# Batch 0's second half of the queries: loaded behind the keys, mixed around the first scores

## The chip, the cores and the metric

The kernel runs on one core of one Trainium2 chip. The metric is the device time in microseconds (us) of one execution; three executions of the kernel before are known, and one more was taken with the hardware profiler. The core has five engines that run side by side and wait for each other by semaphores: TensorE (PE; its weight loads are listed apart as PEld), VectorE (DVE), ScalarE (ACT), GpSimd (POOL) and SyncE (SP). DMA transfers are issued by POOL, by SP and, once, by ACT.

## The reference

Attention within blocks, with keys and values whose blocks were first mixed by a matrix that is normalized by rows and columns five times, and behind it a gated feed-forward network without an expert choice:

```python
P = sort_net                                   # 4 x 8 heads x 8 x 8 blocks
for _ in range(5):
    P = P - max(P, -1); P = exp(P)
    P = P / (sum(P, -1) + 1e-09)
    P = P / (sum(P, -2) + 1e-09)
k_sorted = einsum('bhij,bhjcd->bhicd', P, k_b)  # v_sorted likewise; blocks of 96 rows
scores = q_b @ k_sorted_b.T / sqrt(64)
attn = softmax(scores)
x = (attn @ v_sorted_b), heads side by side     # 3072 x 512
out = (silu(x @ w_gate) * (x @ w_val)) @ w_out  # d_ff 1536
```

q, k and v are 4 x 8 x 768 x 64 in float32; the kernel computes in bfloat16 and accumulates in float32.

## The kernel before

**Stages.** The 3072 output rows are worked in eight pieces `n` of 384 rows (two for each batch). For each piece there are 12 pairs of `gate` and `value` (four matmuls each over 384 columns) and the output matmuls `outp` of the piece before. Between these, PE's order has the attention work of coming pieces: the mixing of keys and queries into their transposed form (`kq_chunk`, for batch 0 `k0_chunk` and `q0_chunk`), the mixing of values (`v_chunk`), the scores (`scores`, 16 small matmuls, followed by exponentials on ACT in `exps`), the product with the values (`av`, whose result is divided on DVE: `r_sb` and `st`) and a transposition (`x_to`).

**Order.** Up to the first two gate and value pairs everything runs in an order written out by hand on PE, POOL, DVE and ACT (first `manual_schedule`): what stands earlier in the program is executed earlier on its engine. After that PE, POOL, ACT and SP keep the written order, which `merge` makes from a list of costs and due times, and DVE is ordered by the framework.

**The start.** POOL issues the loads of batch 0: the values in two halves (`load_v(0, ...)`), the first half of the queries (`load_q0(0)`; a half `t` is four of the eight blocks, in a layout of 128 partitions by 24 rows), and the keys in two halves (`k0`). Then it makes its share of the value copies (`copy_v`), which put the values in an order by head dimension into `vch`. ACT makes the rest of these copies between its exponentials of the five normalizing rounds. POOL then issues the gate and value weights in four column ranges (`load_gv`), with the second half of the queries, `load_q0(1)`, behind the first range, and both halves of batch 1's values; later come three mixing products on POOL (`mix_rows`), four tiny memsets to `pad`, batch 1's keys and queries in halves and the output weights.

**PE's order of the start.** 105 tiny matmuls and some `fill`s (matmuls of zeros with 512 columns), the transposition of the mixing matrix (`w_ps`), `q0_chunk(0, ...)` and `v_chunk(0, ...)` in turns, `k0_chunk`, then the first four scores and value products with single fills between them, the first two gate and value pairs in pieces (`early`), and `q0_chunk(1, ...)`, which mixes the second half of the queries in chunks of 16 and 8. These queries are first read by the fifth score unit, `qk(0, 4)`, which stands behind three more gate and value steps.

**Banks and drains.** A chunk's result stands in a PSUM tile. Tag `gen` has three single banks that are given out in turn, `x` one bank, `a` and `b` two banks each. A chunk ends with a `drain`, a cast to bfloat16 by ACT (`"s"`) or DVE (`"v"`), as the call says:

```python
def q0_chunk(t, at, n, eng, tag):
    ...
    for lc in range(n):
        for two in range(2):
            nc.tensor.matmul(tp[two * D:(two + 1) * D, lc], lhsT=q0[t][:, at + lc, :],
                             rhs=sel[:, two], start=True, stop=True)
    drain(eng, dst[:, :, :, at:at + n], tp.rearrange("p l g r -> p g r l"))
```

A chunk of 8 is 16 matmuls and a drain of 512 columns, a chunk of 16 is 32 matmuls and a drain of 1024 columns.

## Time and profile before

| | |
|---|---|
| three executions | 247.69, 244.64 and 244.58 us, median 244.64 |
| the profiled execution | 244.79 us, of which 243.0 us are the span from its first to its last instruction |
| PE busy | 233.1 us (96% of the span) |
| DVE, ACT, POOL busy | 154.9, 112.5, 54.0 us |
| PE busy from 0 to 12 us | 8.51 us |
| PE busy from 12 to 18 us, and from 18 to 24 us | 5.71 and 5.37 us |
| PE busy from 30 to 60 us | 29.79 us |
| granted TensorE clock | 1.00 |

A time in the profile counts from the first instruction. The views used below are the 40 slices (busy tenths of every engine), the chain of work that ended last in order of time, the timeline (each line: start, duration, engine, line, operation, tiles, count; in brackets the idle time before it and what ended it), and tables by stretches of time (busy time of each engine, granted clock, share of the 16 DMA engines that is busy, and GB/s). Durations of PE are modelled ends, so that neighbouring matmuls overlap in the list.

### The profile page before, as it was taken

How to read it: one execution, taken by the hardware profiler on the slowest of the kernel's cores; microseconds unless marked ns; L12 is line 12 of the kernel's file. 1: busy time of each engine (PE TensorE's matmuls, PEld its weight loads, DVE VectorE, ACT ScalarE, POOL GpSimd, SP SyncE). 2: the span in 40 equal slices, each digit the busy share in tenths (PEclk: the TensorE clock that was granted, in tenths of full speed). 3: DMA queues.
4: the chain of work that ended last, by engine and by line, in shares of the span. 5: the costliest groups of instructions: out<-in, count | busy, mean ns of one | idle time of the engine just before them, and what ended most of it. 6: DMA issues, size and time to landing. Idle time of an engine off the chain costs nothing.

```text
span 243.0 us, 6137 instructions
## 1 busy us (share of the span) xinstructions
PE 233.1 (96%) x2587; PEld 138.8 (57%) x2611; DVE 154.9 (64%) x325; ACT 112.5 (46%) x191; POOL 54.0 (22%) x54
## 2 busy tenths in 40 slices
PE   7799999999999999999999999999999999999993
PEld 5376665676556556555565565565556555555543
DVE  6696889775666585776855765484566477444700
ACT  3987662576525444455454253345226433333221
POOL 5996328970006098000000000000000000000000
PEclk9999999999999999999999999999999999999999
DMA  5999999999926997462122112012102211110122
GB/s 95 211 123 184 207 212 211 206 210 200 182 79 126 203 182 116 95 134 61 42 71 65 35 43 80 0 59 63 44 31 61 60 36 43 43 43 3 43 86 86
DMA packets 40698, 24.77 MB, mean 102 GB/s; under 512 B 29408, under 2 KB 35424, under 8 KB 40672
## 3 DMA queue, kind: packets, MB, share of 16 engines
q0 software_dynamic: 20688, 14.16, 39.8%
q1 hardware_dynamic: 19840, 10.17, 15.9%
q8 instruction: 20, 0.33, 0.6%
q10 hardware_dynamic: 144, 0.07, 0.1%
q14 instruction: 6, 0.05, 0.1%
HBM read 28.32 MB, written 7.86 MB: 149 GB/s over the span
## 4 chain that ended last, share of the span: by engine, by line
PE 90%; DVE 4%; DMA 2%; issue 1%; ACT 1%; DVEq 0%; POOLq 0%
PE v_ps L428 25%; PE g_ps L410 25%; PE o_ps L445 24%; PE av_ps L359 3%; PE tkq L264 3%; PE qk L332 3%; DMA v<-in_v_dram 2%; PE tv L310 1%; PE o_ps L461 1%; PE tv L300 1%; DVE vt L242 1%; PE tk L284 1%; DVE h L433 1%; PE g_ps L561 1%; PE idle_ps L477 1%
## 5 line engine op out<-in xcount | busy, mean ns | idle before, releaser
L420 DVE SCALAR_TENSOR_TENSOR gs_sb<-th_sb,g_ps 128x384 bf16<-128x384 bf16 x96 | 52.9, 552 | 50.3 <-ACT th_sb L418 47.3
L410 PE MATMUL g_ps<-xt,wg_sb 128*128 128x384 bf16 x376 | 76.6, 325 | 0.1
L428 PE MATMUL v_ps<-xt,wv_sb 128*128 128x384 bf16 x376 | 76.5, 326 | 0.0
L418 ACT ACTIVATE th_sb<-g_ps 128x384 bf16<-128x384 f32 x96 | 47.1, 491 | 56.9 <-PE g_ps L410 54.2
L445 PE MATMUL o_ps<-wo,h 128*128 128x512 bf16 x254 | 61.4, 379 | 1.5 <-issue 0.5
L433 DVE SCALAR_TENSOR_TENSOR h<-v_ps,gs_sb 128x384 bf16<-128x384 f32 x96 | 53.4, 556 | 7.8 <-PE tq L274 0.5
L428 PEld LDWEIGHTS <-wv_sb 128*128 128x128 bf16 x376 | 35.0, 97 | 23.1 <-issue 0.2
L410 PEld LDWEIGHTS <-wg_sb 128*128 128x128 bf16 x376 | 34.9, 97 | 23.4
L445 PEld LDWEIGHTS <-h 128*128 128x128 bf16 x276 | 26.1, 98 | 28.5
L450 ACT COPY o_sb<-o_ps 128x512 f32<-128x512 f32 x23 | 13.5, 586 | 49.3 <-PE o_ps L445 49.3
L148 POOL COPY vch<-v 64x1536 bf16<-64x1536 bf16 (+2 forms) x11 | 28.8, 2662 | 9.5 <-PE g_ps L410 7.5
L345 ACT ACTIVATE e_all<-qk 96x768 bf16<-96x768 f32 x30 | 23.2, 801 | 4.3 <-PE qk L332 4.3
L365 DVE TENSOR_TENSOR st<-av_ps,r_sb 96x512 bf16<-96x512 f32 x32 | 21.8, 680 | 0.3
L359 PEld LDWEIGHTS <-e_all 96*128 96x128 bf16 x256 | 12.0, 98 | 4.9 <-ACT e_all L345 0.7
L359 PE MATMUL av_ps<-vt,e_all 96*128 96x65 bf16 x256 | 13.0, 193 | 0.4 <-ACT e_all L345 0.4
L244 ACT CAST vt<-tv 96x1024 bf16<-96x1024 f32 (+1 forms) x11 | 10.1, 931 | 4.4 <-PE tv L310 3.5
L363 DVE RECIPROCAL r_sb<-av_ps 96x8 f32<-96x8 f32 x32 | 6.4, 199 | 7.9 <-PE av_ps L359 7.9
L242 DVE CAST vt<-tv 96x1024 bf16<-96x1024 f32 (+1 forms) x7 | 7.5, 1065 | 1.9 <-PE tv L310 1.8
L242 DVE COPY oq_v<-o_ps 128x128 f32<-128x128 f32 x1 | 0.3, 292 | 9.3 <-PE o_ps L461 9.3
L477 PE MATMUL idle_ps<-warm_sb 128*128 128x512 bf16 x20 | 5.7, 384 | 0.5 <-issue 0.5
L395 POOL DMA_DIRECT2D q_scr<-in_q_dram x2 | 5.6, 2813 | 0.3 <-issue 0.3
L146 ACT COPY vch<-v 64x768 bf16<-64x768 bf16 (+1 forms) x4 | 5.4, 1374 | 0.3 <-DMA v<-in_v_dram 0.3
(89 smaller groups left out, 133.0 us busy)
## 6 DMA issues: line engine op xcount, KB each, us to landing
out_dram<-o_sb SPq DMA_DIRECT2D x23, 256.0 KB, 2.0
v<-in_v_dram POOLq DMA_DIRECT2D x4, 384.0 KB, 12.3
wo<-in_moe_w_out_dram POOLq DMA_DIRECT2D x3, 512.0 KB, 16.2
kqp<-in_k_dram POOLq DMA_DIRECT2D x2, 768.0 KB, 9.8
q_scr<-in_q_dram POOLq DMA_DIRECT2D x2, 768.0 KB, 17.2
v<-in_v_dram POOLq DMA_DIRECT2D x2, 768.0 KB, 9.3
wg_sb<-in_moe_w_gate_dram POOLq DMA_DIRECT2D x2, 512.0 KB, 12.3
wv_sb<-in_moe_w_val_dram POOLq DMA_DIRECT2D x2, 512.0 KB, 14.5
```

Source lines behind the costliest of these rows:

```text
L148: eng.tensor_copy(dst, src.transpose([0, 2, 1]))
L242: nc.vector.tensor_copy(dst, src)
L345: nc.scalar.activation(e_all[:, n:n + 2, 0:4 * C], wide[0:C, :, 0:4 * C], AF.Exp, scale=scale)
L359: nc.tensor.matmul(o[:, two, i4, 0:D + 1], lhsT=e[:, i4 * C:i4 * C + 128], rhs=vt[:, 2 * g + two, half * 4 + i4, 0:D + 1], start=True, sto ...
L365: nc.vector.tensor_tensor(st.rearrange("p i two d -> p two i d"), o[0:C, :, :, 0:D], r_sb.to_broadcast([C, 2, 4, D]), op=ALU.mult)
L410: nc.tensor.matmul(g_ps, lhsT=wg_sb[:, kc, ts(m, 128)], rhs=xt[:, kc, :], start=(kc == 0), stop=(kc == NKC - 1))
L418: nc.scalar.activation(th_sb, g_ps, AF.Tanh, scale=0.5)
L420: nc.vector.scalar_tensor_tensor(gs_sb, th_sb, 1.0, g_ps, op0=ALU.add, op1=ALU.mult)
L428: nc.tensor.matmul(v_ps, lhsT=wv_sb[:, kc, ts(m, 128)], rhs=xt[:, kc, :], start=(kc == 0), stop=(kc == NKC - 1))
L433: nc.vector.scalar_tensor_tensor(h_tiles[n][:, m, :], v_ps, 0.5, gs_tiles.pop(m), op0=ALU.mult, op1=ALU.mult)
L445: nc.tensor.matmul(o_ps, lhsT=h_w[:, m, ts(t3, 128)], rhs=wo_sb[part][:, m % 4, :], start=(m == 0), stop=(m == NFC - 1))
L450: nc.scalar.copy(o_sb, o_ps)
```

## The change

- `load_q0(1)` moves up on POOL: from behind the first weight range to directly behind the keys, ahead of POOL's value copies.
- The value copies on ACT (columns 24 to 60 of the first 60) are cut at 24, 34, 46 and 60 instead of 24, 36, 48 and 60: 10, 12 and 14 columns instead of 12 each.
- The second half of batch 1's values, `load_v(1, 2, 4)`, moves on POOL from behind the first half to behind the first halves of batch 1's keys and queries.
- `pad` has sixteen memsets instead of four.
- On PE the two fills ahead of `qk(0, 0)` and the one ahead of `av(0, 0)` go; in their places stand `q0_chunk(1, 0, 8, "s", "gen")` and `q0_chunk(1, 8, 8, "v", "gen")`. At the old place behind the first gate and value pairs only `q0_chunk(1, 16, 8, "v", "x")` is left; the chunk of 16, with its drain on ACT, goes.

```diff
-    def copy_v(eng, pair, rows, s, n=4, d0=0, d1=D):
-        cs = slice(s * (C // n), (s + 1) * (C // n))
+    def copy_v(eng, pair, rows, s, n=4, d0=0, d1=D, cs=None):
+        cs = cs or slice(s * (C // n), (s + 1) * (C // n))
...
         nc.gpsimd.dma_start(out=k0[rows], in_=k_nat[0, :, a * HC:(a + 1) * HC, :])
+    load_q0(1)
     copy_v(nc.gpsimd, 0, lowr, 0)
     copy_v(nc.gpsimd, 0, lowr, 3)
     copy_v(nc.gpsimd, 0, lowr, 5, 8, 40, D)
     load_gv(0, 256)
-    load_q0(1)
     load_gv(256, 512)
     load_gv(512, 1024)
     load_gv(1024, DF)
     load_v(1, 0, 2)
-    load_v(1, 2, 4)
...
-    pad = const.tile([1, 4], FP32)
+    pad = const.tile([1, 16], FP32)
...
         if it == 2:
-            copy_v(nc.scalar, 0, lowr, 2, 8)
+            copy_v(nc.scalar, 0, lowr, 0, cs=slice(24, 34))
         if it == 3:
-            copy_v(nc.scalar, 0, lowr, 3, 8)
+            copy_v(nc.scalar, 0, lowr, 0, cs=slice(34, 46))
...
-    copy_v(nc.scalar, 0, lowr, 4, 8)
+    copy_v(nc.scalar, 0, lowr, 0, cs=slice(46, 60))
     copy_v(nc.scalar, 0, lowr, 5, 8, 0, 40)
...
-    nc.gpsimd.memset(pad[:, 0:1], 0.0)
-    nc.gpsimd.memset(pad[:, 1:2], 0.0)
-    nc.gpsimd.memset(pad[:, 2:3], 0.0)
-    nc.gpsimd.memset(pad[:, 3:4], 0.0)
+    for n in range(16):
+        nc.gpsimd.memset(pad[:, n:n + 1], 0.0)
     for lo, hi in ((0, 2), (2, 4)):
         load_k(1, lo, hi)
         load_q(1, lo, hi)
+        if lo == 0:
+            load_v(1, 2, 4)
...
-    fill(pair_tile("idle_ps", "b")[:, 0:512], 2)
+    q0_chunk(1, 0, 8, "s", "gen")
     qk(0, 0, "a")
     qk(0, 1, "b")
-    fill(bank_tile("idle_ps"), 1)
+    q0_chunk(1, 8, 8, "v", "gen")
     av(0, 0, "a")
...
     value_out(0, 1, first[3])
-    q0_chunk(1, 0, 16, "s", "b")
     q0_chunk(1, 16, 8, "v", "x")
```

## The prediction

> **What bounds the kernel now.** I read the slices first, then the chain of work that ended last, then the timeline and the DMA tables of the stretch that the diff touches.

> ```profile
> PE   7799999999999999999999999999999999999993
> DMA  5999999999926997462122112012102211110122
> ```

> PE is full from about 12 us on; only what makes PE start sooner, or stand less, before about 43 us can move the end. DMA is nearly full from 6 to 65 us, so a hole there matters too. The chain, in order of time (start, duration, what):

> ```profile
> 11.79 0.62 PE tq L274 x32
> 12.42 0.35 PE tv L300 x8
> ...
> 13.49 1.23 DVE vt L242
> 14.72 0.04 issue
> 14.76 1.71 PE tk L284 x96
> ...
> 17.66 0.82 ACT e_all L345
> ...
> 24.68 0.64 PE tq L274 x32
> 25.32 0.01 issue
> 25.34 0.56 DVE h L433
> 25.89 0.47 DVE gs_sb L420
> ...
> 27.02 0.61 DVE kqt L242
> 27.63 0.05 issue
> 27.67 0.51 PE qk L332 x16
> ```

> Between 12 and 28 us the chain leaves PE again and again: casts on DVE, the first exponential on ACT, and at the end four DVE steps (`h`, `gs_sb`, `h`, the cast `kqt`), for which the fifth scores wait. Behind 27.67 it is nearly all PE.

> ```profile
> 9.38 2.86 POOL L148 COPY vch<-v 64x1536 bf16<-64x1536 bf16 x1 [0.24 <-DMA v<-in_v_dram]
> 24.61 0.95 PE L274 MATMUL tq<-sel,qk 128*64 128x64 bf16 x48
> 22.05 0.61 POOL L100 DMA_DIRECT2D v<-in_v_dram  x1 [1.71 <-DMA qk<-in_q_dram]
> 13.50:14.00 0.50, 0.50 (x24) 0.41 (x20) 0.50 (x1) 0.50 (x2) 0.50 (x2) 1.00 0.06 12
> 15.00:15.50 0.50, 0.50 (x44) 0.50 (x39) 0.31 (x2) 0.50 (x1) 0.50 (x1) 1.00 1.23 154
> ```

> The last two lines end with the DMA share and GB/s: from 12.5 to about 14.8 us the DMA engines are nearly idle.

> **Part 1, the value copies.** In the third normalizing round ACT's copy of 12 columns (6.29 us, 1.52 long) is in the way of the next exponential, which starts 0.46 after the DVE product before it (7.25 to 7.71) where the other rounds show 0.25 to 0.26. Ten columns are 640 elements: between the rows of 768 (1.50) and 480 (1.00) that is about 1.28, so the copy ends 0.24 sooner and the rounds gain 0.20. The two later copies grow by the same total, from 768 to 896, ending at about 11.95 as now. But the first value mixing (`tv`, 12.35) also needs POOL's second copy, which waits for the values' second half and ends at 9.38 + 2.86 = 12.24; nothing in the diff moves it. The last matmul of `tq` starts at 12.22, so copy and PE arrive together today, and the 0.20 turns into a wait for POOL. I take 0; bounds 0 and -0.05.

> **Part 2, the queries' load.** Its issue (0.57 on POOL) moves from 14.36 to 4.6, where POOL stands 1.71 before its first copy: free. The landings of POOL's first five loads stand in order of issue at 6.27, 9.33, 10.71, 12.59 and 14.42 us, 1.4 to 3.1 apart. In the trace's semaphore records a load arrives in sixteen parts, and one part is late: the keys' second half has fifteen by 13.64 and the last at 14.42. The new load follows the keys at 14.42 + 1.4 to 1.9 = 15.8 to 16.3 (bound: the largest spacing, 3.07, gives 17.5). It is wanted at 16.87 (below). The keys, wanted at 14.56, are ahead of it. Their first half had a load right behind it and their second had none, and both took the same (spacings of 1.88 and 1.83), so I take no delay for them; bound: half of the 0.78 by which the late part lags, of which 0.2 is hidden behind the DVE cast that ends at 14.72, so +0.2. The transfer fills the hole; every later load comes about 2 us sooner. The waits of POOL's loads name each time the load eight places before (22.05: the eighth is these queries), so POOL's order also moves up: with 0.54 less of issue the first value half goes out at 18.85, the mixings end at 20.6.

> **Part 3, memsets and batch 1's values.** A memset starts 0.036 after the one before: 12 x 0.036 = 0.43 on POOL. The next load is then issued at about 21.2 instead of 24.00 and lands 17 later behind a full queue; the 0.43 is hidden. Without that cover it would be 0.43 on loads that have over 2 us of room. Moving the second value half behind two loads of 1.75 each, and 2 us up, puts it at about 40.4 instead of 39.2; POOL's copies would then start at about 36.2 instead of 38.03, and need it after two of 2.8, at 41.8. Free. Batch 1's first queries land at about 38 instead of 42.64. There the trace shows a wait: the matmuls of the gate end their issue at 42.53, the key mixing `tkq` starts at 42.78 behind a wait that ends at 42.67; the two other places leave 0.1 between. **Gain 0.14.**

> **Part 4, the first chunk in place of two fills.** It takes the `gen` bank of the second ACT cast of `tk`, which ends at 16.83; so it starts at 16.87 and, at 0.25 for 16 matmuls (a third of the 48 in 24.61 to 25.36), ends its issue at 17.12, where the fills (two of 0.213) ended at 17.18. The scores behind it keep their 17.28. Its cast is new on ACT ahead of the first exponential: ready at 17.32, 0.59 long, and the next may start 0.10 before its end (ACT's rows overlap so). The exponential starts at 17.83 instead of 17.66: **loss 0.16**. From there ACT, `av` and the DVE row `r_sb`, `st` (18.98 to 22.42 without a gap) hand it on to 24.61. Bounds: 0, if the bank came 0.2 sooner, and 0.3. [...]

> **Part 5, the second chunk in place of one fill.** It waits for the DVE cast that ends at 17.98, and runs to 18.28, inside PE's idle stretch before `av` (18.53, now 18.69). Its DVE cast, 18.49 to 19.17, ends where the first reciprocal can start (19.15). Taken as 0; if the bank only comes with DVE's second cast (18.32), the reciprocal slips to 19.42, 0.27 more.

> **Part 6, 32 matmuls and a 1.01 us ACT cast less at 24.61.** PE saves 32 x 0.016 = 0.51. But the fifth scores wait for DVE: from the start of the first `h` (25.34) it is 2.33 to 27.67, unchanged. That `h` stood 0.52 idle, put down to `tq`. If it is the end of the chunk that frees it, it starts at 24.61 + 0.16 + 0.25 + 0.20 = 25.22, 0.12 sooner. If it waits only for its inputs: 24.92 + 0.16 = 25.08, 0.26 sooner. If the stall is a fixed 0.46 that has nothing to do with the chunk: 25.50, 0.16 later. I take the middle one, which follows the row: **gain 0.12**, the loss of part 4 included. PE then stands up to 0.5 before the fifth scores; that is where most of the 0.51 goes.

> **Sum.** -0.12 - 0.14 = -0.26; by part 6 alone the ends are -0.40 and +0.02, and with the other parts' ends -0.61 (parts 1 and 4) and +0.63 (parts 2, 4 and 5). Span 243.0 to 242.74, profiled execution 244.79 to 244.53. The median of the three runs is 0.15 below the profiled one: 244.64 - 0.26 = **244.4 us**.

> **The clock, a rival.** The granted clock is 1.00 in every stretch, also from 18.00 to 18.50, where PE is busy for 0.12 of 0.50. The change takes 0.64 of fills out of 16.7 to 18.0 and puts 0.51 of matmuls in; from 17.0 to 20.4 PE is busy for 2.99 of 3.40. If the clock fell to half there for that long, those 2.99 would take 5.98, less the 0.41 idle: +2.5, 247.0 us. [...] **2 in 100.**

> **Other rivals.**
> - *PE's whole saving passes*: `h` has more room than the chain shows, and ACT's cast hides. -0.51 - 0.14, with up to 0.15 from part 1 if the values' half lands early: about 243.9. For it: PE is the chain from 28 us on. Against it: the row of DVE steps without a gap. **15 in 100.**
> - *No change*: the stall at `h` stays, or the second chunk's cast slips (part 5): 0.16 - 0.14 or -0.26 + 0.27, about 244.65. For it: the inputs of that `h` were ready at 24.86, so the chunk may not be its cause. **22 in 100.**
> - *Slower: the queries' second half lands late.* PE executes in order, so the first scores stand behind the first chunk. It decides from 16.87 on, and the sum turns positive at about 17.1. With the spacing of 3.07 the chunk starts at 17.55; its cast at 18.01; the exponential at 18.50, +0.84 instead of +0.16; in all -0.26 + 0.68 = +0.42: 245.1. The late sixteenth part speaks for it, the three other spacings against it. **11 in 100.** That the move does nothing because the queue takes the loads in another order is part of this.

> **How the numbers follow.** The forecast has 50 in 100. 243.8 to 245.1 takes in the rivals but the clock and runs beyond them; the likeliest one's own range is 244.2 to 244.7. About 2% (4.9 us) is what a measurement of this kernel can tell from no change: all cases lie within it. I leave 0.02 for faster, 0.03 for slower (the clock, and disturbances like the run of 247.69), 0.95 for the same.

> **What would show it.** The queries landing before 16.6; `tq` at 16.9 and 18.0; a cast of 512 before the first exponential, which starts at 17.8; the reciprocal at 19.15; 16 matmuls at about 24.8; the first `h` at 25.1 to 25.2 and the fifth scores at 27.4 to 27.6 with PE idle before them; `tkq` without a wait for a DMA. An exponential later than 18.1, or scores later than 27.8, would make the forecast wrong; scores before 27.2 would show the larger gain.

## The result: 246.05 us, 0.5% slower, outside the range

The changed kernel takes 246.05 us (median of 12 runs), the kernel before 244.81 on the same chip (12 runs); the ratio is 1.0054, 95% interval 1.0033 to 1.0074. Forecast were 244.4 us and a range of 243.8 to 245.1. That the difference is within 2% was right; its sign was wrong. The profiled execution takes 245.88 us, its span is 244.1 instead of 243.0.

The slices of the changed kernel that answer to the two shown of before (the digits are busy tenths of TensorE, PE, and of the DMA engines):

```profile
PE   7777999999999999999999999999999999999994
DMA  5999999999825999534121212012111211110122
```

The third digit of the DMA row was a 9 both times, though the page's row of GB/s has 123 there before and 191 now. The table by stretches for the hole that the prediction spoke of ends with DMA share and GB/s; the first of these two lines is the kernel before, the second the changed one:

```profile
12.50:14.80 2.30, 2.16 (x75) 2.05 (x74) 2.24 (x4) 2.07 (x4) 2.30 (x4) 1.00 0.23 33
12.50:14.80 2.30, 1.89 (x65) 1.68 (x61) 2.24 (x4) 2.07 (x4) 2.30 (x4) 1.00 1.00 191
```

The hole is filled: 191 GB/s in place of 33. Now the chain of work that ended last, of the changed kernel, in order of time (start, duration, what):

```profile
14.92 1.49 PE tk L283 x83
16.41 0.83 issue
17.24 0.38 PE tk L283 x13
17.62 0.34 PE tv L299 x8
17.96 0.39 PE tq L273 x16
18.35 0.02 issue
18.38 0.59 ACT kqt L243
18.96 0.71 ACT e_all L344
...
23.62 0.14 issue
23.76 0.34 PE x_ps L375 x4
...
26.34 0.57 DVE gs_sb L419
...
27.00 0.56 DVE h L432
...
28.68 0.61 DVE kqt L241
```

Before, `tk` was one piece, `14.76 1.71 PE tk L284 x96`. Now it is broken behind 83 of its 96 matmuls, and 0.83 us are "issue": time in which PE waited for nothing that the profile shows. The timeline shows a second place of this kind (last bracket: idle time and what is named as having ended it):

```profile
14.92 1.49 PE L283 MATMUL tk<-rmix,qk 128*64 128x64 bf16 x83 [0.53 <-DMA qk<-in_k_dram]
17.24 0.38 PE L283 MATMUL tk<-rmix,qk 128*64 128x64 bf16 x13 [0.83 <-issue]
23.76 0.34 PE L375 MATMUL x_ps<-ident,st 96*128 96x96 bf16 x4 [0.70 <-DVE st L364]
```

The last of these is put down to VectorE's third `st`, but that one had ended at 22.78 (22.09 and 0.69 in the chain), a microsecond earlier: something else held PE.

PE's offset against the kernel before (the start of the same step now, less its start then) shows where the time goes: -0.23 us at the last normalizing round (10.11 to 9.88), +0.15 at `tk`, +1.15 at the value mixing behind it, +1.19 at the first `av`, +2.06 at the third `x_ps`, +1.66 at the fifth scores, +1.49 at `tkq` and +1.48 with the last store. (The span grows only by 1.1, as the profiled run of before happens to have 0.4 more behind its last store.) So two stops of PE make the loss, and a late key transfer a little of it.

### The profile page after: what moved, and what is told of

It is laid out like the page before. It is cut to its first block, busy times and chain, and to the rows that moved or that the text cites. A ratio compares the mean times of both kernels' runs of the same rounds, so it can differ in the third digit from the quotient of the medians.

```text
span 244.1 us, 6144 instructions
## 1 busy us (share of the span) xinstructions
PE 232.8 (95%) x2584; PEld 138.8 (57%) x2608; DVE 155.3 (64%) x326; ACT 112.2 (46%) x191; POOL 54.4 (22%) x66
## 4 chain that ended last, share of the span: by engine, by line
PE 87%; DMA 4%; DVE 3%; issue 2%; POOL 1%; ACT 1%; DVEq 0%; POOLq 0%
PE v_ps L427 25%; PE g_ps L409 25%; PE o_ps L444 24%; DMA qk<-in_k_dram 4%; PE av_ps L358 3%; PE tkq L263 3%; PE qk L331 3%; DVE st L364 1%; PE tv L309 1%; PE o_ps L460 1%; PE tv L299 1%; PE tk L283 1%; DVE h L432 1%; DVE gs_sb L419 1%; PE x_ps L375 0%
## 5 line engine op out<-in xcount | busy, mean ns | idle before, releaser
L449 ACT COPY o_sb<-o_ps 128x512 f32<-128x512 f32 x23 | 13.5, 586 | 49.3 <-PE o_ps L444 49.3
L148 POOL COPY vch<-v 64x1536 bf16<-64x1536 bf16 (+2 forms) x11 | 28.9, 2659 | 9.4 <-DMA v<-in_v_dram 9.4
L146 ACT COPY vch<-v 64x640 bf16<-64x640 bf16 (+3 forms) x4 | 5.5, 1394 | 0.2 <-DMA v<-in_v_dram 0.2
## 6 DMA issues: line engine op xcount, KB each, us to landing
q_scr<-in_q_dram POOLq DMA_DIRECT2D x2, 768.0 KB, 18.1
```

The costliest lines, as they stand in the source:

```text
L148: eng.tensor_copy(dst, src.transpose([0, 2, 1]))
L449: nc.scalar.copy(o_sb, o_ps)
```

## What stops PE: its instructions

The page of the kernel before lists a queue that the prediction passed over. In the DMA table it has 20 packets of together 0.33 MB, 16 KB each:

```profile
q8 instruction: 20, 0.33, 0.6%
```

The trace has the times of these packets. In the kernel before one runs from 13.45 to 14.54 us; in the changed one it runs from 14.86 to 15.82. The DMA tables of the stretch from 13.4 to 14.6 us (queue, kind: packets, MB, share; above 100% the packets' times overlap) show it, first those of before:

```profile
q0 software_dynamic: 37, 0.02, 18.7%
q8 instruction: 1, 0.02, 5.7%
```

then the changed kernel, whose table has one line and no instruction packet:

```profile
q0 software_dynamic: 88, 0.25, 106.3%
```

I counted PE's instructions in the trace (matmuls, weight loads and the few recorded semaphore instructions, in order of start). PE stops behind number 704, whose row starts at 16.21 us, and goes on at 17.24, 1.42 us after the packet has landed; it stops again behind number 959, which starts at 22.74, and goes on at 23.76, 1.39 after the end of the next packet (21.48 to 22.37). The two are 255 recorded instructions apart (a few records can be missing). The trace of the changed kernel has 5,204 PE instructions; if the 20 packets carry them all, that is 260 to a packet.

**Theory 1** says: PE's instructions come in blocks of about 255, the distance of the two stops, through the same DMA engines as the data. That the fetch of the block from 704 on is asked for when PE enters the block before it is my estimate, from times: 255 numbers ahead, number 449 starts at 13.15 us before and 12.91 after. In the kernel before the fetch meets nearly empty engines (DMA share 0.23 from 12.5 to 14.8 us) and starts 0.30 later; in the changed one the queries stand in its way (share 1.00), and it starts 1.95 later. PE, which works off small matmuls at this place, runs dry. The second stop follows from the first and from the two chunks: PE enters the block from 704 on at 17.24 instead of 16.06, the next fetch starts 4.24 us later (3.67 before), both times in full engines (DMA share 1.32 from 17.2 to 21.4 us, before 1.24 from 16.0 to 19.7), and the chunks bring number 959 from 24.7 us forward to 22.7.

**Rivals**: the stop belongs to its place (the keys, their buffer, a bank); the twelve memsets or the later values of batch 1 make it; or the early queries themselves do, by order or buffer.

In the kernel before PE doesn't stop at number 704 (`tk` is one piece of 1.71 us); here the first stop costs 1.00 us and the second about 0.87 (worked out below).

## The experiments

Each ratio is against the kernel before, measured again on the same chip as the experiment. Experiments 1 and 5 edit the kernel before, all others the changed kernel.

**1. The load alone.** The kernel before, with only the queries' second half moved behind the keys:

```diff
         nc.gpsimd.dma_start(out=k0[rows], in_=k_nat[0, :, a * HC:(a + 1) * HC, :])
+    load_q0(1)
...
     load_gv(0, 256)
-    load_q0(1)
```

> The kernel before with one edit: the load of the queries' second half behind the keys; PE's order, copies, memsets and the values' halves as before. Theory 1 (PE's instructions arrive by DMA, 16 KB at a time; the load fills the hole in the DMA queues that let one such fetch through at 13.45 us, the fetch comes about 1.4 us later, and PE runs out of instructions): PE stands still for 0.5 to 1 us inside the key mixing tk with no semaphore to wait for, and the second such stop follows near 22 to 24 us; tk itself starts 0.1 to 0.4 later than 14.76 because the keys' late part lands at about 14.8; time 0.8 to 1.8 above the kernel before. Rival (the loss comes from PE's new order: chunks in place of fills, a cast ahead of the exponential): no stop, tk at 14.76, time equal to before within 0.2.

Measured: 245.7 us, ratio 1.0027 (1.0017 to 1.0038). The fetch starts at 14.92, PE stops behind number 705 in the same place:

```profile
14.98 1.49 PE L284 MATMUL tk<-rmix,qk 128*64 128x64 bf16 x83 [0.41 <-DMA qk<-in_k_dram]
17.37 0.38 PE L284 MATMUL tk<-rmix,qk 128*64 128x64 bf16 x13 [0.91 <-issue]
```

Moving the load is enough for the first stop. The second one, which I had expected too, doesn't come, and the loss of 0.76 us is just under the 0.8 to 1.8 expected: the next fetch ends at 22.87, and without the two chunks number 960 comes only at 25.98 us.

**2. All but the load's place.** The changed kernel, with the load behind GpSimd's three copies, ahead of the first weights:

```diff
-    load_q0(1)
     copy_v(nc.gpsimd, 0, lowr, 0)
     copy_v(nc.gpsimd, 0, lowr, 3)
     copy_v(nc.gpsimd, 0, lowr, 5, 8, 40, D)
+    load_q0(1)
     load_gv(0, 256)
```

> The changed kernel with the load of the queries' second half issued behind POOL's copies, ahead of the weights, so that the DMA queues are empty from 12.5 to 14 us again; all else as changed. Theory 1: the fetch starts near 13.4, the stop in tk is gone, the keys land at 14.4; the queries land at 16.3 to 17.3 and the first chunk waits 0 to 0.5 for them; time 0.5 to 1.2 below the changed kernel, near or a little below the kernel before. Rival (PE's order is to blame): time as the changed kernel, 245.6 to 246.

Measured: 244.97 us, ratio 0.9999 (0.9984 to 1.0015). The fetch starts at 13.47, both stops are gone, and the queries, which land at 17.36, make the first chunk wait:

```profile
14.76 1.71 PE L283 MATMUL tk<-rmix,qk 128*64 128x64 bf16 x96
17.41 0.44 PE L273 MATMUL tq<-sel,qk 128*64 128x64 bf16 x16 [0.61 <-DMA qk<-in_q_dram]
```

The wait of 0.61 is a little more than the 0 to 0.5 expected. The stops are worth more: the ratio is 0.0055, or 1.3 us, below the changed kernel's. With experiment 1 this shows that the second stop takes both, the first stop and the chunks: either alone doesn't make it.

**3. More instructions ahead.** The changed kernel with 121 instead of 105 tiny warming matmuls, that is 32 PE instructions more ahead of all the rest:

```diff
-    dots(105)
+    dots(121)
```

> The changed kernel with 121 instead of 105 of the tiny matmuls at the start, 32 PE instructions more. Theory 1: the stop sits at a fixed count of PE instructions, so it comes 32 instructions (16 matmuls with their weight loads) earlier in the program: tk stops with about 29 of its 96 matmuls left instead of 13; the second stop moves too; time as the changed kernel within 0.5. Rival (the stop is a wait of the last tk chunk for a bank or a load): the stop stays with 13 matmuls left.

Measured: the stops move up the program by 32 instructions. The first comes behind 67 of `tk`'s matmuls instead of 83 (29 are left), the second in an `av` instead of `x_ps`:

```profile
16.82 0.64 PE L283 MATMUL tk<-rmix,qk 128*64 128x64 bf16 x29 [0.99 <-issue]
23.87 0.29 PE L358 MATMUL av_ps<-vt,e_all 96*128 96x65 bf16 x2 [2.33 <-issue]
```

A stop that keeps its number and changes its place doesn't belong to keys, buffers or banks. The time was to stay within 0.5 us of the changed kernel and didn't: 248.86 us, ratio 1.0154 (1.0137 to 1.0172). The table by stretches shows why (duration, PE busy, granted clock, DMA share, GB/s):

```profile
18.92:22.34 3.42, 2.09 (x48) 1.00 1.34 190
22.34:29.17 6.83, 5.30 (x34) 0.50 1.24 206
29.17:32.00 2.83, 2.83 (x32) 1.00 1.24 214
```

The second stop came 1.4 us earlier, lasted 2.33, and the clock fell to half for 6.83 us.

**4. The memsets and batch 1's values undone.** The changed kernel with four memsets, and both halves of batch 1's values at their old place:

```diff
-    for n in range(16):
+    for n in range(4):
         nc.gpsimd.memset(pad[:, n:n + 1], 0.0)
...
     load_v(1, 0, 2)
+    load_v(1, 2, 4)
...
-        if lo == 0:
-            load_v(1, 2, 4)
```

> The changed kernel with four memsets and with batch 1's second value half at its old place behind the first; all else as changed. Theory 1: both stops stay, time as the changed kernel within 0.4. Rival (the memsets or the later load disturb the start): time falls by 0.5 or more.

Measured: 246.21 us, ratio 1.0045 (1.0028 to 1.0062), as the changed kernel. Both stops are there, at 16.13 to 17.07 and 22.57 to 23.86. These parts are not the cause.

**5. Bytes that nobody reads.** The kernel before with a spare load right behind the keys: the same queries once more, into a tile that the output weights fill later. Nothing is moved:

```diff
         nc.gpsimd.dma_start(out=k0[rows], in_=k_nat[0, :, a * HC:(a + 1) * HC, :])
+    nc.gpsimd.dma_start(out=wo_sb[2].rearrange("p a b -> p (a b)")[:, 0:QC * D], in_=q_runs[0, 1])
```

> The kernel before with one more load, which nothing reads: behind the keys the same 128 rows of the queries' second half are also loaded into the tile of the last output weights, which the later load of these weights overwrites. Nothing else is moved. Theory 1: the hole in the queues is filled, the fetch starts at 14.5 to 15 us, TensorE stops in tk at instruction 704 until 1.4 us after the fetch's end, and the time is 0.8 to 1.5 us above the kernel before (245.4 to 246.1 us). Rival (the order of the queries' own load, its buffer or its readers make the stop, not the bytes in the queues): no stop, 244.6 to 244.9 us.

Measured: 245.85 us, ratio 1.0039 (1.0014 to 1.0064). The fetch starts at 14.41, a little sooner than expected, and the stop at number 704 is shorter:

```profile
14.84 1.49 PE L285 MATMUL tk<-rmix,qk 128*64 128x64 bf16 x83
16.70 0.38 PE L285 MATMUL tk<-rmix,qk 128*64 128x64 bf16 x13 [0.37 <-issue]
```

So it is the bytes in the queues and neither the queries' order, nor their buffer, nor who reads them. (The profile is that of the fastest of the ten runs, 245.39 us; in it PE ends 0.47 later than before. What the other runs have more is not shown.)

**6. Fewer instructions ahead.** The changed kernel with 32 of the tiny matmuls replaced by two wide fills, 60 instructions fewer:

```diff
-    dots(105)
-    fill(idle_ps, 2)
+    dots(73)
+    fill(idle_ps, 4)
```

> The changed kernel with 32 of the 105 small warming matmuls replaced by two wide ones of about the same time, so 60 TensorE instructions fewer ahead of all that follows. Theory 1: the stop is at a fixed instruction number, so it moves 60 instructions down the program, out of tk and into the first query chunk tq; the fetch still starts near 14.9 us, so the stop ends near 17.2 us as before but TensorE has done 60 instructions more by then: stop of 0.4 to 0.7 us in place of 1.0. The second stop moves past the first x_ps, to a place reached after its fetch has ended, and is gone. The time is 244.8 to 245.5 us. Rival (the stop belongs to the place in tk, that is to the keys or the buffers there): the stop stays in tk behind 83 of its matmuls, 245.6 to 246.2 us.

Measured: the first stop moves 60 instructions down, as expected, out of `tk` and into `tq`, and the second is gone. (It ends at 17.89 and not near 17.2: PE enters the block before later, and the fetch starts at 15.42.) But the time is 247.6 us, ratio 1.0103 (1.0069 to 1.0137), far above the 245.5 that I expected at most. PE's offset against before is +0.53 at 25.5 us and +2.59 at 92.8, because a later border has moved too, into a row of small matmuls:

```profile
17.89 0.29 PE L273 MATMUL tq<-sel,qk 128*64 128x64 bf16 x7 [0.58 <-issue]
91.87 1.17 PE L263 MATMUL tkq<-rmixp,kqp 128*64 128x64 bf16 x62
94.98 0.22 PE L263 MATMUL tkq<-rmixp,kqp 128*64 128x64 bf16 x2 [1.94 <-issue]
```

At about 89 us PE enters the block before; from 88.7 to 92.6 every slice of the DMA engines is full, a 9 in all 40 (the queries of the later batches, which land at 94.72, an output store and two transfers into `xt`), the fetch runs from 92.70 to 93.67, and PE goes on 1.31 us later. This block, most of it mixing, had lasted only 4 us. Behind it the granted clock is 0.50 from 96.29 to 99.70. Shifting all borders mended one stop and made another.

**7. The parts that have nothing to do with the queries.** The changed kernel with the queries' load and PE's order as before; the value copies, the memsets and batch 1's later values stay:

```diff
-    load_q0(1)
     copy_v(nc.gpsimd, 0, lowr, 0)
...
     load_gv(0, 256)
+    load_q0(1)
...
-    q0_chunk(1, 0, 8, "s", "gen")
+    fill(pair_tile("idle_ps", "b")[:, 0:512], 2)
...
-    q0_chunk(1, 8, 8, "v", "gen")
+    fill(bank_tile("idle_ps"), 1)
...
+    q0_chunk(1, 0, 16, "s", "b")
     q0_chunk(1, 16, 8, "v", "x")
```

> The changed kernel without its three steps about the queries: their second half is loaded where the kernel before loads it and mixed where it was mixed before (two fills ahead of the first scores, one behind them, sixteen columns at the end). What stays of the change: the value copies dealt out anew, twelve more memsets, batch 1's last values loaded later. Theory 1 (TensorE runs out of instructions because the queries' load closes the hole in the queues through which the fetch passes): no stop in tk at instruction 704 and none at 960, the fetch again starts near 13.5 us; left over are the shorter wait at tkq (0.14 us by the trace of before) and, if the keys' late sixteenth part lands no later than before, up to 0.24 us from the earlier first values: 244.2 to 244.6 us, against 244.6 before. Rival (the new dealing of the value copies or the memsets cost time of their own): 245 us or more.

Measured: 244.6 us against 245.06 of before on that chip, ratio 0.9986 (0.9967 to 1.0006); no stop. The rival's 245 us or more is not seen; whether anything is gained can't be told from the times. The trace has PE 0.10 later from the first `tv` on (which waits 0.18 for GpSimd's copy, as Part 1 foresaw) and 0.05 earlier from `tkq` on, so 0.15 at that wait. The 0.24 us from earlier first values didn't come.

**8. Load and mixing apart.** The changed kernel with the load behind the copies, the two fills back ahead of the first scores, one chunk of 8 ahead of the first `av` and 16 columns at the old place:

```diff
-    load_q0(1)
     copy_v(nc.gpsimd, 0, lowr, 0)
...
+    load_q0(1)
     load_gv(0, 256)
...
-    q0_chunk(1, 0, 8, "s", "gen")
+    fill(pair_tile("idle_ps", "b")[:, 0:512], 2)
...
-    q0_chunk(1, 8, 8, "v", "gen")
+    q0_chunk(1, 0, 8, "v", "gen")
...
-    q0_chunk(1, 16, 8, "v", "x")
+    q0_chunk(1, 8, 16, "s", "b")
```

> The changed kernel with the queries' second half loaded behind GpSimd's three value copies and ahead of the first weights, the two fills put back ahead of the first scores, the first eight columns mixed behind the second scores (in place of the one fill) and sixteen columns at the end. Theory 1: fetch near 13.5 us, no stop in tk, no wait for the queries as they land near 17.4 us and are wanted at about 18; first exponential at 17.4 to 17.7 us as before, fifth scores about 0.4 us before the 27.67 us of the kernel before, tkq less its wait: 244.1 to 244.5 us. Rival (no order of these steps is worth anything here, since the stage from the first scores to the first h is bound by VectorE and ScalarE and not by TensorE): fifth scores within 0.1 us of before, 244.5 to 244.7 us.

Measured: 243.9 us, ratio 0.9957 (0.9943 to 0.9971): faster than the kernel before, and than the changed one. The fetch starts at 13.61, no stop. In the chain PE no longer leaves for `h` and `kqt` ahead of the fifth scores:

```profile
24.70 0.62 PE tq L273 x32
25.32 0.76 PE g_ps L409 x4
26.08 0.65 PE v_ps L427 x4
26.73 0.65 PE g_ps L409 x4
27.38 0.45 PE qk L331 x16
```

PE's offset against before is +0.02 at the first scores, -0.36 at the fifth and -0.61 at `tkq`. So the rival (no order of these steps is worth anything) doesn't hold.

## Why the prediction was wrong, step by step

The sum was -0.26 us; PE's own end moved by +1.48. From the offsets, the terms between: +0.15 up to `tk`, +1.00 for the first stop, +0.05 up to the first exponential, +0.46 from there to the fifth scores, -0.17 at `tkq`. Experiment 2, which has no stop, gains 0.41 from the first exponential to the fifth scores (9.60 us instead of 10.01); so the second stop, net of that, cost about 0.46 + 0.41 = 0.87 (an estimate from three profiles).

**The step that failed** is in Part 2: "The transfer fills the hole; every later load comes about 2 us sooner." I booked the hole as free. It was the path of the fetch at 13.45 us, and I didn't read the queue of 20 packets in the DMA table. The first stop costs 1.00 and the second 0.87 us, together 1.87. Sum and result are 1.74 apart, so all other steps together were better than forecast by 0.13. In the kernel before, PE passed number 704 only 1.5 us after the fetch had ended, and the stops end 1.25 to 1.5 us after it: there was hardly any slack, and none of this can be seen in a view of waits.

**Part 1 (nothing gained) held** in experiments 2, 4 and 8, whose first `tv` starts at 12.35 or 12.36 like before, and not in this run. Here the first `tv` starts at 12.11 instead of 12.35, because GpSimd's second copy found the values' second half there without a gap; in experiment 4, with the same order of loads, it waits 0.36 us for them.

**Part 2, the other statements.** The queries landed at 16.21, inside 15.8 to 16.3. "I take no delay for them", the keys, was wrong: their last sixteenth part lands at 14.78 instead of 14.42, while the other fifteen are there at 13.60 (13.64 before). `tk` starts 0.15 later than before, within the bound of 0.2; in this run it took back the front's 0.24.

**Parts 3, 4 and 5 held.** The wait at `tkq` is gone, 0.17 for a forecast of 0.14. From the first chunk to the first exponential 0.97 us pass (17.41 to 18.38 in experiment 2, 17.89 to 18.86 in the changed kernel), forecast 0.96. The second chunk costs nothing: from the exponential to `av` 0.86, before 0.87.

**Part 6 was too small.** Three readings of the stall at `h` stood side by side and I took the middle one (7.39 us from the first exponential to `h`). Experiments 2 and 8 both show 7.27; the reading that `h` waits for its inputs alone had 7.25. That is 0.12 more gain than taken.

**The clock, "2 in 100", was weighed wrong, and its price came out by luck.** Of the changed kernel's twelve runs five take 247.1 to 247.5 us with a mean clock of 0.984 to 0.993; the other seven take 245.6 to 246.15 with 0.998 to 1.0. I worked out 247.0 for that case, but as 2.5 us on top of 244.5; measured are about 1.3 (medians 247.18 and 245.84) on top of a time that the stops had already raised. The weight was an estimate from a count of PE's busy time in which no stop existed; the fall to half was an assumption there, and experiment 6 shows one (0.50 from 96.29 to 99.70 us). The stops aren't needed for it, either: experiment 2 has none, and three of its twelve runs show a mean clock of 0.993 and 245.7 to 245.9 us, where the other nine take 244.4 to 245.2.

**The rival "queries land late"** has its price at the exponential confirmed by experiment 2 (+0.72 with the chunk at 17.41; the prediction had +0.84 with it at 17.55), and not its total: PE's end moves by +0.14 there, for a forecast of +0.42. It isn't what happened.

**The chances.** "Same" within 2% with 0.95 was right. The range was too narrow by 0.95 us, for it summed only waits that the trace of before shows.

## What to carry to other kernels

Before a transfer is moved into a hole of the DMA queues, list everything that passes through that hole, instruction fetches included (here 20 packets of 16 KB): find their times, the instruction numbers at which the engine would run dry, and how long before it the fetch ends. A long row of small matmuls behind full queues is where this decided here (ahead of the changed kernel's stops a block lasted 3.3 us, 12.91 to 16.21, and 5.5 us, 17.24 to 22.74; in full engines PE went on 6.5 us after it had entered the block before, 17.24 to 23.76); an idle time put down to "issue" (0.83 us), or to an engine long done (0.70 us), was its sign. The gain was had by keeping the transfer out of that hole: experiment 8 leaves the load behind the copies and mixes only what is wanted early, and is about 1.0 us faster than the kernel before (0.43% of 245).
